# Moving eight conditioning columns from TensorE to VectorE, and three re-timings around them

## The chip, the cores and the metric

One core of a Trainium2 chip. The metric is device time of one launch in microseconds (us), median over runs. A chunk is 512 of the 2048 rows. TensorE is the matrix engine (PE in the profile, PEld its weight load), VectorE is DVE, ScalarE ACT, GpSimd POOL, SyncE SP.

## The reference, cut to what matters

```python
mod = (silu(c) @ w_mod)            # 6 vectors of 1024: sa, ca, ga, sb, cb, gb
h = layernorm(x) * (1 + ca) + sa
x = x + ga * attention(h)          # 32 query heads, 4 key/value heads, last 512 keys
h = layernorm(x) * (1 + cb) + sb
x = x + gb * swiglu(h)
```

`x` is 2048 x 1024 in bf16. Every one of the six vectors is eight columns of 128 in the layout on the chip. The change is about `ga`, the gate of the attention output, first used when the output projection of the first half ends, some 265 us into the run.

## The kernel before

Attention runs in 64 head steps for each half of the rows, numbered 0 to 63 and 64 to 127. A step `i` projects a query, computes the scores of step `i - 1`, and multiplies the probabilities of step `i - 2` with the values. Each step has one softmax reciprocal on VectorE (L824), which serves below as its time mark. In the steps up to 20 the projection is a plain product; later ones use a seven-product scheme whose sums load VectorE. Small work is hung on the steps:

```python
def mod_mm(w_ap, wbuf, k, cols):           # a column of mod: weights 128x128 times one column
    for n, (j, o) in enumerate(cols):
        mm(bank(XB, 1, 2 * o), w_ap[:, j * P:(j + 1) * P], sc_bf[:, k:k + 1], ...)

def load_mt(n):                            # a 128-column block of w_mod, turned by the DMA crossbar
    T.op(Q_mt[n % 2], lambda: SP.dma_start_transpose(mt[n % 2]..., w_mod[:, (NF + n) * P:(NF + n + 1) * P]), ...)

def mod_col(n):                            # the same column on VectorE: multiply by silu(c), sum
    T.op(DVE, lambda: V.scalar_tensor_tensor(mt[n % 2], mt[n % 2], 1.0, sc_row, ..., accum_out=mcol[:, n:n + 1]), ...)

def row_task(dst, dbuf, src, sbuf):        # 8 columns -> a row on all partitions, in three parts
    ...                                    # 4 ScalarE diagonals, then twice: 4 matmuls, a VectorE copy

# in pre0(i), the beginning of step i of the first half:
if i in (8, 9):
    load_wga(i - 8)                        # plain loads, 1 MB each, for the columns of ga
if i in (8, 9):
    for dt in range(4 * (i - 8), 4 * (i - 8) + 4):
        modulate(hT[1], B_hT[1], dt, 0, 0, B_mode, x1_tiles)
...
if i == 5:
    bgx.append(row_task(sc_row, B_scr, sc_bf[:, :], B_sc))
for k in {12: (0, 1, 2), 13: (3, 4, 5), 14: (6, 7)}.get(i, ()):
    mod_mm(wga[:, k, :], B_wga[k], k, GCOLS)
```

The output projection issues the big load of summed weights (`wo_sum`, 2 MB) after its first product, and lets background work, the normalization of the next rows, run between products:

```python
for ch in (2, 3):
    bg.append(ln_task(ch, 0, 0, B_mode))   # normalize a tile (L427), turn it by DMA; two tile buffers
o_phase(0, o_hook0)                        # o_hook0 runs one part of bg at a time

def hk(idx, j):                            # in o_phase
    if j == TPC - 1 and idx < 4:
        load(idx + 2)                      # idx 0: the first wo_sum load
```

The softmax here doesn't subtract the row's maximum and nothing guards it: scores larger than these inputs give would overflow.

## Time and profile before

| | before |
|---|---|
| median, range | 1160.27 us, 1159.91 to 1160.35 (3 runs) |
| TensorE busy | 1148.3 us, 99% of the span |
| VectorE busy | 817.4 us, 71% |
| weighted sums on VectorE (L603) | 24, 29.2 us |

The busy table tells who can set the time; the waits of TensorE, one by one, tell where anything is to be had besides its own work. Line numbers are those of each kernel: L805, L824, L827, L835, L956, L603 and L1122 before are L792, L811, L814, L822, L943, L590 and L1109 after.

### The profile page before, as it was taken

Reading aid. Unit: us, or ns where it says so; the run is one execution under the profiler, and the core shown is the slowest. Engines: PE = TensorE matmul, PEld = TensorE weight load, DVE = VectorE, ACT = ScalarE, POOL = GpSimd, SP = SyncE. Lnnn points to the kernel's source line nnn. Section 1 sums busy time; section 2 is a strip of 40 time slices with the busy share of each in tenths; the row PEclk is TensorE's granted clock in tenths of the full one; section 3 lists DMA queues with packets and bytes.
Section 4 is the critical chain, followed back from the end, with each engine's and each line's share of the span. In section 5 each row is a group of like instructions: output and inputs, shape, how many; then the busy total and the mean of one; then the engine's idle time right before and its main releaser. Section 6 shows DMA issues by size and latency. Waiting matters only on the chain.

```text
span 1158.3 us, 18250 instructions
## 1 busy us (share of the span) xinstructions
PE 1148.3 (99%) x7105; PEld 588.0 (51%) x7105; DVE 817.4 (71%) x1638; ACT 532.7 (46%) x745; POOL 68.4 (6%) x137
## 2 busy tenths in 40 slices
PE   8999999999999999999999999999999999999999
PEld 5565556654445666656444444444444444444444
DVE  4858897757567777686567898777558777776536
ACT  3867777731127777787110354454110444544110
POOL 1100221100000111111000010000000000000000
PEclk9999999999999999999999999999999999999999
DMA  9679999976807898844875332323774424234443
GB/s 330 145 181 207 225 217 211 236 182 194 242 3 183 197 194 204 203 94 119 191 198 165 87 95 73 108 75 100 209 201 143 121 73 109 73 98 131 130 160 109
DMA packets 289941, 179.98 MB, mean 155 GB/s; under 512 B 130496, under 2 KB 278080, under 8 KB 289856
## 3 DMA queue, kind: packets, MB, share of 16 engines
q1 hardware_dynamic: 226880, 92.31, 35.5%
q10 hardware_dynamic: 54336, 55.05, 15.0%
q0 software_dynamic: 8640, 31.46, 9.3%
q8 instruction: 56, 0.92, 0.3%
q14 instruction: 29, 0.24, 0.1%
HBM read 128.45 MB, written 19.92 MB: 128 GB/s over the span
## 4 chain that ended last, share of the span: by engine, by line
PE 96%; DVE 2%; ACT 1%; DMA 1%; issue 0%; SPq 0%; ACTq 0%; DVEq 0%
PE ps L272 96%; ACT arena L805 1%; DMA arena<-in_A_wq_dram 1%; DVE arena L835 1%; DVE arena L906 0%; DVE st L413 0%; SPq L341 0%; SPq L310 0%; PE ps L276 0%; ACT arena L618 0%; DVE arena L852 0%; ACT tmp L743 0%; DVE arena L1566 0%; ACT L1551 0%; DVE arena L827 0%
## 5 line engine op out<-in xcount | busy, mean ns | idle before, releaser
L272 PE MATMUL ps<-arena 128*128 128x512 f16 (+2 forms) x6800 | 1141.2, 330 | 7.0 <-POOL arena L406 2.2
L272 PEld LDWEIGHTS ps<-arena 128*128 128x128 bf16 (+1 forms) x6800 | 577.8, 98 | 563.0 <-DVE arena L835 6.2
L805 ACT ACTIVATE arena<-ps 128x1024 bf16<-128x1024 f32 x256 | 261.5, 1022 | 44.6 <-PE ps L272 32.8
L838 ACT ACTIVATE tmp<-ps 128x512 f32<-128x512 f32 x167 | 99.7, 597 | 295.9 <-PE ps L272 280.8
L906 DVE TENSOR_TENSOR arena<-arena 128x512 f16<-128x512 bf16 x328 | 133.3, 419 | 3.0
L835 DVE TENSOR_TENSOR arena<-ps,tmp 128x512 bf16<-128x512 f32 (+1 forms) x134 | 91.8, 685 | 49.3 <-PE ps L272 37.8
L838 ACT ACTIVATE nsc<-ps 128x512 f32<-128x512 f32 x84 | 50.1, 596 | 93.2 <-PE ps L272 90.9
L827 DVE TENSOR_TENSOR arena<-ps,rl 128x512 f16<-128x512 f32 x128 | 88.5, 691 | 4.9 <-DVE rl L824 0.5
L835 DVE TENSOR_TENSOR arena<-ps,nsc 128x512 f16<-128x512 f32 x84 | 57.3, 687 | 41.2 <-PE ps L272 30.0
L824 DVE RECIPROCAL rl<-ps 128x4 f32<-128x4 f32 x128 | 23.1, 180 | 87.1 <-PE ps L272 86.2
L1551 ACT ACTIVATE arena<-arena 128x512 f16<-128x512 f16 x84 | 49.9, 624 | 32.4 <-DVE arena L835 32.4
L1122 DVE TENSOR_TENSOR tmp<-ps,tmp 128x512 f32<-128x512 f32 x32 | 22.1, 690 | 58.5 <-ACT tmp L838 48.8
L1046 DVE TENSOR_TENSOR arena<-arena 128x2048 f16<-128x2048 f16 (+3 forms) x56 | 56.0, 1010 | 9.3 <-PE ps L272 8.8
L838 ACT ACTIVATE arena<-ps 128x512 f32<-128x512 f32 x16 | 9.6, 597 | 90.5 <-PE ps L272 90.5
L956 DVE TENSOR_TENSOR arena<-arena 128x512 f16<-128x512 bf16 x120 | 47.9, 419 | 2.0 <-DMA arena<-in_A_wo_dram 0.9
L413 DVE BATCH_NORM_STATS2 st<-x_res 128x6 f32<-128x512 bf16 x58 | 39.5, 682 | 3.7 <-DMA x_res<-in_A_x_dram 3.5
L1566 DVE TENSOR_TENSOR arena<-arena 128x512 f16<-128x512 f16 x84 | 35.0, 416 | 0.3
L1123 DVE TENSOR_TENSOR tmp<-tmp,rowb 128x512 f32<-128x512 f32 (+1 forms) x49 | 33.7, 687 | 1.7
L427 DVE TENSOR_SCALAR nsc<-x_res,mv,rstd 128x1024 f16<-128x1024 bf16 (+1 forms) x30 | 16.2, 539 | 23.3 <-DMA arena<-nsc 22.4
L603 DVE SCALAR_TENSOR_TENSOR arena<-arena 128x1024 bf16<-128x1024 bf16 x24 | 29.2, 1215 | 0.0
L1124 DVE TENSOR_TENSOR arena<-tmp,x_res 128x512 bf16<-128x512 f32 (+1 forms) x33 | 22.3, 676 | 1.1
L835 DVE TENSOR_TENSOR arena<-ps,rowb 128x512 f16<-128x512 f32 x28 | 19.3, 690 | 3.9 <-ACT rowb L838 3.4
(87 smaller groups left out, 333.4 us busy)
## 6 DMA issues: line engine op xcount, KB each, us to landing
arena<-in_A_wq_dram SPq DMA_DIRECT2D x28, 512.0 KB, 5.3
arena<-wo_sum ACTq DMA_DIRECT2D x7, 2048.0 KB, 8.6
arena<-in_B_w_gate_dram SPq DMA_DIRECT2D x28, 512.0 KB, 4.0
arena<-in_B_w_up_dram SPq DMA_DIRECT2D x28, 512.0 KB, 5.1
arena<-wd_sum ACTq DMA_DIRECT2D x8, 1792.0 KB, 7.8
arena<-in_B_w_down_dram ACTq DMA_DIRECT2D x6, 1792.0 KB, 7.1
arena<-in_A_wo_dram POOLq DMA_DIRECT2D x16, 512.0 KB, 4.8
wo_sum<-arena POOLq DMA_DIRECT2D x16, 512.0 KB, 4.6
```

The costliest lines, as they stand in the source:

```text
L272: T.op(PE, lambda: TE.matmul(out_ap, lhsT, rhs, start=start, stop=stop, skip_group_check=skip), reads=reads, writes=[bank_buf])
L413: T.op(DVE, lambda: V.bn_stats(st_[sl][:, hf * 6:hf * 6 + 6], x_res[:, t, hf * 512:hf * 512 + 512]), reads=[B_x[t]], writes=[B_st[sl]])
L805: T.op(ACT, lambda: A.activation(ex_s[es][:, 2 * kp:2 * kp + 2, :], banks2(SCB + 2 * kp), AF.Exp, scale=att_scale), writes=[PB[SCB + 2 * k ...
L827: T.op(DVE, lambda: V.tensor_tensor(o_s[os_].rearrange("p (a b) d -> p a b d", a=2), psap(PVB * 512, [[512, 2], [130, 2], [1, P]]), rlb, A ...
L835: T.op(DVE, lambda: V.tensor_tensor(out, bank(ba), other, ADD), reads=[ob2], writes=[PB[ba], ob])
L838: T.op(ACT, lambda: A.activation(dst, bank(bk), AF.Copy), writes=[PB[bk], db])
L906: T.op(st, lambda: eng.tensor_tensor(o, a, b, op), reads=rd, writes=[wr])
L956: T.op(DVE, lambda: V.tensor_tensor(o, a, b, SUB), reads=rd, writes=[wr])
L1046: T.op(DVE, lambda: V.tensor_tensor(o, a, b, SUB), reads=rd, writes=[sb])
L1123: T.op(DVE, lambda: V.tensor_tensor(tm, tm, rw, MULT), reads=[B_row[row]], writes=[tb])
L1551: T.op(ACT, lambda: A.activation(o, s_, AF.Silu), reads=[sb], writes=[ob])
L1566: T.op(DVE, lambda: V.tensor_tensor(gu[blk][:, p, :], o, s_, MULT), reads=[sb, ob], writes=[B_gu[blk][p]])
```

## The change

Its intent: TensorE sets the time, so the 64 one-column matmuls for `ga` go; `ga` is computed like the other late columns, from crossbar-turned weights and VectorE sums, placed in steps where VectorE has room. The row of silu(c) that these sums need is spread at step 8 instead of 5, chunk 1 is scaled six tiles then two, and the `ga` row is spread later.

```diff
-            NF = NE + DT
-            NL = NJ - NF
+            NL = NJ - NE
...
-            LOADT = {14 + 4 * n: n for n in range(NL)}
+            TAKES = [12, 17, 61] + [i for i in range(15, 2 * NI - 15) if i % 4 == 3 or (i > NI + 2 and i % 4 == 2 and i % 5 in (1, 4))]
+            TAKES = sorted(TAKES)[:NL]
+            TAKET = {i: n for n, i in enumerate(TAKES)}
+            LOADT = {max(i - 4, TAKES[max(n - 2, 0)] if n > 1 else 0): n for i, n in TAKET.items()}
...
-                        mod_take(g0, B_late[g0 + 1])
-                        if g0 == 1:
+                        mod_take(g0, B_late[g0])
+                        if g0 == 0:
+                            bgx.append(row_task(rowb[0], B_row[0], mod_bf[:, 2 * DT:3 * DT], B_late[0]))
+                        elif g0 == 2:
...
-                if i in (8, 9):
-                    load_wga(i - 8)
...
-                    for dt in range(4 * (i - 8), 4 * (i - 8) + 4):
+                    for dt in range(6 * (i - 8), 6 if i == 8 else DT):
...
-                if i == 5:
+                if i == 8:
                     bgx.append(row_task(sc_row, B_scr, sc_bf[:, :], B_sc))
-                for k in {12: (0, 1, 2), 13: (3, 4, 5), 14: (6, 7)}.get(i, ()):
-                    mod_mm(wga[:, k, :], B_wga[k], k, GCOLS)
```

More of the change, by code (lines that the diff above doesn't have):

```diff
@@ L188, in bass_adaLN_cond__sliding_block_cached__swiglu_ffn__prompt_kernel @@
     c6 = S_("c6", [P, DT], F32)
-    mcol = S_("mcol", [P, 3 * DT], F32)
+    mcol = S_("mcol", [P, 4 * DT], F32)
     gain = [S_("gain%d" % i, [P, DT], BF16) for i in range(2)]
@@ L572, in _ @@
             norm(2, 2, 2, 512, 512)
-            B_wga = [_Buf("wga%d" % k) for k in range(DT)]
-            wga = arena.at(OFF_OT[3], [DT, D], BF16, B_wga)
-            GCOLS = [(j, j) for j in range(DT)]
-            def load_wga(i):
-                T.op(dq("q_wga%d" % i), lambda: SP.dma_start(
-                    wga[:, i * HK:(i + 1) * HK, :],
-                    w_mod[i * HK * P:(i + 1) * HK * P, NE * P:NE * P + D].rearrange("(k p) n -> p k n", p=P)),
-                     writes=B_wga[i * HK:(i + 1) * HK])
-            NF = NE + DT
-            NL = NJ - NF
+            NL = NJ - NE
             B_mt = [_Buf("mt%d" % i) for i in range(2)]
@@ L598, in load_mt @@
                 T.op(Q_mt[n % 2], lambda: SP.dma_start_transpose(
-                    mt[n % 2].rearrange("p (a b) -> p a b", a=1), w_mod[:, (NF + n) * P:(NF + n + 1) * P]),
+                    mt[n % 2].rearrange("p (a b) -> p a b", a=1), w_mod[:, (NE + n) * P:(NE + n + 1) * P]),
                      writes=[B_mt[n % 2]])
@@ L607, in mod_take @@
             def mod_take(g0, cbuf):
-                T.op(DVE, lambda: V.tensor_copy(mod_bf[:, NF + g0 * DT:NF + (g0 + 1) * DT], mcol[:, g0 * DT:(g0 + 1) * DT]),
+                T.op(DVE, lambda: V.tensor_copy(mod_bf[:, NE + g0 * DT:NE + (g0 + 1) * DT], mcol[:, g0 * DT:(g0 + 1) * DT]),
                      reads=[B_mcol], writes=[cbuf])
@@ L1194, in _ @@
             LOADX = {14: 2, 20: 3}
-            LOADT = {14 + 4 * n: n for n in range(NL)}
+            TAKES = [12, 17, 61] + [i for i in range(15, 2 * NI - 15) if i % 4 == 3 or (i > NI + 2 and i % 4 == 2 and i % 5 in (1, 4))]
+            TAKES = sorted(TAKES)[:NL]
+            TAKET = {i: n for n, i in enumerate(TAKES)}
+            LOADT = {max(i - 4, TAKES[max(n - 2, 0)] if n > 1 else 0): n for i, n in TAKET.items()}
+            assert len(TAKES) == NL and len(LOADT) == NL and not {NI, NI + 1} & (set(TAKET) | set(LOADT))
             take_oT(0)
@@ L1220, in mods @@
             def mods(i):
-                if i - 5 in LOADT:
-                    n = LOADT[i - 5]
+                if i in TAKET:
+                    n = TAKET[i]
                     mod_col(n)
@@ L1225, in mods @@
                     if last == DT - 1:
-                        mod_take(g0, B_late[g0 + 1])
-                        if g0 == 1:
+                        mod_take(g0, B_late[g0])
+                        if g0 == 0:
+                            bgx.append(row_task(rowb[0], B_row[0], mod_bf[:, 2 * DT:3 * DT], B_late[0]))
+                        elif g0 == 2:
                             mod_gain(1, B_late[2], B_g[1])
-                        elif g0 == 2:
+                        elif g0 == 3:
                             bgx.append(row_task(rowb[1], B_row[1], mod_bf[:, 5 * DT:6 * DT], B_late[3]))
@@ L1271, in pre0 @@
                     next(x1_stats[1])
-                if i == 5:
+                if i == 8:
                     bgx.append(row_task(sc_row, B_scr, sc_bf[:, :], B_sc))
-                for k in {12: (0, 1, 2), 13: (3, 4, 5), 14: (6, 7)}.get(i, ()):
-                    mod_mm(wga[:, k, :], B_wga[k], k, GCOLS)
-                    if k == DT - 1:
-                        T.op(DVE, lambda: V.tensor_copy(mod_bf[:, NE:NF], psap(XB * 512, [[2, DT]])), writes=[PB[XB], B_late[0]])
-                        bgx.append(row_task(rowb[0], B_row[0], mod_bf[:, NE:NF], B_late[0]))
                 if i == ND + 2:
```

## The prediction

> **What bounds the kernel now.** I read three views, in this order: the page's busy table and chain that ended last (which engine sets the end), then TensorE's timeline of the first 125 us (where that engine is held up, and by whom), then the timeline of all engines from 45 to 80 us (what the others do there). The page first:
>
> ```profile
> span 1158.3 us, 18250 instructions
> ...
> PE 1148.3 (99%) x7105; PEld 588.0 (51%) x7105; DVE 817.4 (71%) x1638; ACT 532.7 (46%) x745; POOL 68.4 (6%) x137
> ...
> PE 96%; DVE 2%; ACT 1%; DMA 1%; issue 0%; SPq 0%; ACTq 0%; DVEq 0%
> ```
>
> TensorE is busy 99% of the span and carries 96% of the last chain. So a change can save only two things: work that TensorE itself does, and the few moments in which it stands. TensorE's timeline of the early attention steps shows both:
>
> ```profile
> 47.53 0.60 PE L272 MATMUL ps<-arena 128*128 128x512 bf16 x2 [0.24 <-ACT arena L805]
> 48.65 6.09 PE L272 MATMUL ps<-arena 128*128 128x512 bf16 x54 [0.51 <-ACT arena L805]
> 55.20 11.90 PE L272 MATMUL ps<-arena 128*128 128x512 f16 x88 [0.46 <-DVE arena L432]
> 66.94 0.74 PE L272 MATMUL ps<-sc_bf,arena 128*128 128x1 bf16 x24
> 67.55 3.66 PE L272 MATMUL ps<-arena 128*128 128x512 bf16 x28
> 71.04 0.74 PE L272 MATMUL ps<-sc_bf,arena 128*128 128x1 bf16 x24
> 71.64 3.66 PE L272 MATMUL ps<-arena 128*128 128x512 bf16 x28
> 75.14 0.54 PE L272 MATMUL ps<-sc_bf,arena 128*128 128x1 bf16 x16
> 75.54 23.79 PE L272 MATMUL ps<-arena 128*128 128x512 bf16 x198
> ```
>
> Columns: start, duration, instruction, count, and in brackets the idle time before it with what ended it. The reader is to see the 24+24+16 = 64 one-column matmuls (output 128x1), which are the gate columns and which the change deletes; two waits on ScalarE's exponential (L805) at 47.5 and 48.7; and one wait at 55.20 on the scaling of chunk 1 (L432, `modulate`). The all-engine timeline says what stands behind them:
>
> ```profile
> 45.29 1.28 ACT L618 ACTIVATE arena<-arena,c 128x128 bf16<-128x128 bf16 x4
> ...
> 46.48 2.12 ACT L805 ACTIVATE arena<-ps 128x1024 bf16<-128x1024 f32 x2
> ...
> 48.49 1.27 ACT L618 ACTIVATE arena<-arena,c 128x128 bf16<-128x128 bf16 x4
> ...
> 51.02 0.68 DVE L626 CAST arena<-ps 128x512 bf16<-128x512 f32 x1
> 51.62 1.37 DVE L432 TENSOR_SCALAR arena<-arena,gain,mod_bf 128x512 f16<-128x512 f16 x4
> ...
> 54.13 0.69 DVE L827 TENSOR_TENSOR arena<-ps,rl 128x512 f16<-128x512 f32 x1
> 54.74 1.42 DVE L432 TENSOR_SCALAR arena<-arena,gain,mod_bf 128x512 f16<-128x512 f16 x4
> ```
>
> The L618 rows are the diagonals of the conditioning row (`row_task`), the L626 row its copy: they sit in ScalarE's and VectorE's queues ahead of exponentials and scalings. VectorE does four scalings in step 8 and four in step 9, the latter only after its softmax division (L827); TensorE needs them at once.
>
> **What the Trainium skill says.** "TensorE: Matmul & The Clock Gate", section "Back-to-back issue gap", gives an issue floor of about 25 ns for matmuls of 1 to 64 columns. The trace agrees: 67.55 - 66.94 = 0.61 us for 24, 25.4 ns each. The 163 ns that a row shows as the mean of one is latency, not cost. "VectorE: DVE Perf Modes", section "The perf-mode tier table", lists 2x for tensor_tensor on bf16 in SBUF but has no row for scalar_tensor_tensor with an accumulated sum; here one over 1024 elements takes 1215 ns (L603, 24 of them, 29.2 us), plus 82 ns to read the sum. "Advanced Engine Details and Errata", section "X-Bar Transpose (TRN2)", says transposing DMAs are as fast as plain ones; here a crossbar load of one 256 KB weight column block lands 4.4 us (median, 3.1 to 10.8) after issue, a plain 256 KB load of the same weights 6.5, so nothing contradicts it.
>
> **The change, part by part.**
>
> 1. Gate columns off TensorE. 64 matmuls go. The pitch of an attention step, read from one softmax reciprocal to the next in the timeline, is 3.50 us without columns (58.42, 61.92, 65.42) and 4.09, 4.10 and 3.90 us with them (69.51, 73.61, 77.51). 0.59 + 0.60 + 0.40 = **1.59 us**, 24.8 ns each, all on the path.
>
> 2. The same columns on VectorE: 8 more weighted sums of 1.215 + 0.08 us = 10.4 us, and one 0.17 us copy in place of the one removed. By the diff's formula the 32 sums fall in steps 12, 15, 17, then 19, 23, 27 and so on; against before the new places are 12, 15, 17, 61, 74, 86, 94, 106. I compared each with VectorE's busy time in that step: steps 12 to 18 hold 1.6 to 3.1 us of 3.5, and step 17 loses the old row copy as well; step 61 has 1.6 of 2.6; steps 74, 86, 94, 106 have about 2.1 of 3.5, so 3.4 after. The steps where VectorE is truly full (23 to 42; five small TensorE waits on L835 lie there) keep exactly the sums they had. Hence about **0**, and I allow 0.1 us. The change deletes 2 MB of plain loads at steps 8 and 9 and adds eight 256 KB crossbar loads, the same bytes spread out. Every sum comes at least four steps (11.6 us or more, by the reciprocals of steps 59 and 63) after its load was placed, against a slowest landing of 10.8: hidden, but not by much in the steps with short pitch.
>
> 3. First conditioning row (`sc_row`) from steps 5 to 7 to steps 8 to 10. Its 8 small matmuls cost the same 0.44 us anywhere (a step with four of them is 3.72 instead of 3.50). What changes is ScalarE. TensorE's start-to-start pitch at the two waits exceeds the normal 0.21 us by 0.41 and 0.68, 1.09 us together. Without the diagonals the two exponentials (2.13 us) still limit the short step 7: replaying the queue, the exponential at 46.48 begins at about 45.75 and the second half of the next scores at 47.9 instead of 48.65, of which 0.22 is moved row work. Gain **0.54 us**, not 1.09. At steps 8 to 10 ScalarE has 1.36 us free per 3.5 us step against diagonals of 1.28 to 1.48: no new wait.
>
> 4. Six scalings in step 8, two in step 9. At 55.20 and the next three matmul groups starts slip by 0.63 + 0.11 + 0.11 + 0.16 = 1.01 us, because four scalings at 0.34 us each run after the division. With six done earlier (2.06 us, and the copies at 47.93 and 51.02 gone from VectorE's queue) only two run late; I replay them ending 0.24 us after TensorE would want the last. Gain **0.78 us**. The crossbar transposes that feed the scalings land by 48.2, before they would start at about 50.1.
>
> 5. Gate row (`rowb[0]`) from steps 14 to 16 to steps 40, 44, 48. Same matmuls. ScalarE has 10.6 us of work per 13.1 us group there, so 1.48 us fits, but tightly within one step. The copy of eight columns (0.17 us) at step 39 lands where VectorE is full: cost **0.2**, with 0.1 more for ScalarE.
>
> Sum: 1.59 + 0.54 + 0.78 - 0.1 - 0.3 = 2.5 us. I take 2.4: 1160.27 - 2.4 = **1157.9 us**, 0.2%.
>
> **Rivals.**
> *VectorE becomes the wait.* 10.4 us more work on an engine that TensorE does wait for. For it: step 111, where a sum, its copy and statistics meet, is followed by a 0.44 us wait on L835. Against: the new places have room on paper. If each of the five second-half and late places cost such a wait, 2.2 us go back: about 1160.
> *Only the matmuls count.* If ScalarE's two exponentials hold the early short steps anyway and the scalings stay late behind something I missed, such as the transposes, parts 3 and 4 give nothing: 1160.27 - 1.6 + 0.4 = 1159.1.
> *Crossbar loads crowd the DMA queues.* DMA is 95 to 100% busy between 78 and 245 us. A late load stalls VectorE's in-order queue and then TensorE: 1 to 3 us, so up to 1161. Against: only 2 of the extra loads fall after 210 us in chunk 0, and no TensorE wait there names a DMA.
> *More than predicted.* If all waits of parts 3 and 4 vanish: 1.59 + 1.09 + 1.01 = 3.7, about 1156.6. Against: the two exponentials of 2.13 us do not fit the short step.
>
> **Range and chances.** Ends of the range: nearly everything of parts 3 and 4 gained and nothing lost (1156.8), and only the matmuls with small VectorE losses (1159.2). Runs of before spread over 0.44 us, so the machine adds little. 2% would be 23 us; the whole stretch that changes holds no such sum. Same: 0.99.
>
> **What would show it.** In the profile after: no one-column matmuls between 66 and 76 us and reciprocals 3.50 us apart there (part 1); 32 rows of L603's kind (39 us) with no new wait on L835 near steps 61, 74, 86, 94, 106 (part 2); one wait of about 0.4 to 0.6 us on the exponential near 48 us, not two (part 3); the wait on the scaling at about 0.25 us (part 4); the wait on L835 near step 40 grown by about 0.2 us (part 5). A wait of VectorE on the crossbar loads, or several waits on L835 in the second chunk, would make it wrong.

## The result, and the profile after

The changed kernel takes 1158.79 us (median of 6, 1157.90 to 1159.89) against 1160.31 us before in the same rounds (1159.84 to 1160.84). The ratio is 0.9988, 95% interval 0.9975 to 1.0000. Ratios here are the mean time of one kernel's fast runs over that of the other's of the same rounds, so not quite the ratio of the medians. That is 1.5 us where 2.4 was predicted, inside the range.

The page of the changed kernel, its busy line and one of its groups:

```profile
PE 1147.0 (99%) x7041; PEld 586.2 (51%) x7041; DVE 826.1 (71%) x1654; ACT 532.7 (46%) x745; POOL 69.1 (6%) x137
...
L590 DVE SCALAR_TENSOR_TENSOR arena<-arena 128x1024 bf16<-128x1024 bf16 x32 | 38.9, 1215 | 0.0
```

64 matmuls are gone (7105 to 7041) and eight sums came (24 to 32). TensorE's timeline from 40 to 125 us, then the lines of its continuation from 125 to 172 us (start, duration, what, count, idle time before and what ended it):

```profile
...
42.27 5.44 PE L272 MATMUL ps<-arena 128*128 128x512 bf16 x48 [0.16 <-ACT arena L792]
48.17 48.15 PE L272 MATMUL ps<-arena 128*128 128x512 bf16 x392 [0.46 <-ACT arena L792]
96.79 11.14 PE L272 MATMUL ps<-arena 128*128 128x512 bf16 x98 [0.46 <-ACT arena L792]
...
```

```profile
...
149.01 17.02 PE L272 MATMUL ps<-arena 128*128 128x512 f16 x140 [0.66 <-DVE arena L822]
166.23 5.96 PE L272 MATMUL ps<-arena 128*128 128x512 f16 x46 [0.20 <-DVE arena L822]
```

Before, TensorE's timeline from 125 to 175 us is one row:

```profile
124.83 50.53 PE L272 MATMUL ps<-arena 128*128 128x512 f16 x407
```

The reader is to see that the stretch which held two waits, the scaling wait and the columns is now one unbroken row of 48 us with one wait ahead of it, and that new or larger waits stand at 149 and 166 us. To see what each is worth, I lined up the softmax reciprocals of equal steps in the two traces:

| stretch (reciprocals of steps) | before, us | after, us | difference |
|---|---|---|---|
| start to 4 | 41.24 | 41.52 | +0.28 |
| 4 to 20 | 57.69 | 54.41 | -3.28 |
| 20 to 34 | 45.33 | 45.36 | +0.03 |
| 34 to 46 | 39.89 | 41.13 | +1.24 |
| 46 to 65 | 60.88 | 60.87 | -0.01 |
| 65 to 66 (holds the output projection) | 102.89 | 103.40 | +0.51 |
| 66 to 129 | 206.28 | 206.18 | -0.10 |
| 129 to the end | 604.09 | 604.08 | -0.01 |

So the change gains 3.28 us by step 20 and gives 1.75 us back at two places far from it (0.44 of it are the gate row's own matmuls, which moved from steps 14 to 16 to steps 40 and 44). The start is not the change's: both kernels are the same there, and it lay between -0.4 and +1.8 us of before in later traces (TensorE's first matmuls wait for a load, and its first half-size ones sometimes run at 213 ns instead of 109). I therefore compare traces from the reciprocal of step 4 to the end of the span: 1117.05 us before, 1115.43 after.

The timeline of VectorE around the first place given back, changed kernel, 141 to 151 us:

```profile
143.58 0.88 DVE L943 TENSOR_TENSOR arena<-arena 128x512 f16<-128x512 bf16 x2 [0.34 <-DMA arena<-in_A_wo_dram]
...
144.99 1.21 DVE L590 SCALAR_TENSOR_TENSOR arena<-arena 128x1024 bf16<-128x1024 bf16 x1
146.12 0.08 DVE L590 DVE_READ_ACCUMULATOR arena<-arena 128x1 f32 x1
146.24 0.17 DVE L595 CAST mod_bf<-mcol 128x8 bf16<-128x8 f32 x1
```

The copy of the eight finished columns (L595) sits in a step in which VectorE has no room, and here the weight sums (L943) also came late, as a weight load held VectorE for 0.34 us.

The second place, in the output projection. All-engine timelines, before (252 to 270 us) and after (250 to 268 us):

```profile
251.73 18.51 PE L272 MATMUL ps<-arena 128*128 128x512 bf16 x85
...
252.84 0.54 DVE L427 TENSOR_SCALAR nsc<-x_res,mv,rstd 128x1024 f16<-128x1024 bf16 x1
...
259.36 0.55 DVE L427 TENSOR_SCALAR nsc<-x_res,mv,rstd 128x1024 f16<-128x1024 bf16 x1 [0.74 <-DMA arena<-nsc]
...
264.00 0.55 DVE L427 TENSOR_SCALAR nsc<-x_res,mv,rstd 128x1024 f16<-128x1024 bf16 x1 [1.70 <-DMA arena<-nsc]
264.46 0.68 DVE L1122 TENSOR_TENSOR tmp<-ps,tmp 128x512 f32<-128x512 f32 x1
...
```

```profile
254.06 0.54 DVE L427 TENSOR_SCALAR nsc<-x_res,mv,rstd 128x1024 f16<-128x1024 bf16 x1
...
262.62 0.55 DVE L427 TENSOR_SCALAR nsc<-x_res,mv,rstd 128x1024 f16<-128x1024 bf16 x1 [2.78 <-DMA arena<-nsc]
...
265.93 0.68 DVE L1109 TENSOR_TENSOR tmp<-ps,tmp 128x512 f32<-128x512 f32 x1
...
266.67 1.69 PE L272 MATMUL ps<-arena 128*128 128x512 f16 x7 [0.32 <-DVE tmp L1109]
```

The third normalization (L427) needs the tile buffer of the first, which its transpose still reads. In the changed kernel that transpose landed later, VectorE stood 2.78 us there, and its sum L1109 released TensorE's bank (the buffer that its next product goes to) late. The kernel before also waits on such transposes, 0.74 and then 1.70 us, without cost to TensorE. Against step 65, its first normalization (L427) starts at 7.8 us and its sum L1122 at 19.4; in the changed kernel these are 10.8 and 22.6. So VectorE's later start, after the last attention transposes, makes most of the difference between these two traces; whether it is needed for the wait is tested below. The question for the experiments: which part of the change does this, and is it chance?

### The profile page after: what moved, and what is told of

Its sections match the earlier page's. It is cut to its first block, busy times and chain, and to the rows that moved or that the text cites. A ratio compares the mean times of both kernels' runs of the same rounds, so it can differ in the third digit from the quotient of the medians.

```text
span 1156.9 us, 18141 instructions
## 1 busy us (share of the span) xinstructions
PE 1147.0 (99%) x7041; PEld 586.2 (51%) x7041; DVE 826.1 (71%) x1654; ACT 532.7 (46%) x745; POOL 69.1 (6%) x137
## 4 chain that ended last, share of the span: by engine, by line
PE 95%; DVE 2%; DMA 1%; ACT 1%; issue 1%; SPq 0%; DVEq 0%; ACTq 0%
PE ps L272 95%; DMA arena<-nsc 1%; DVE arena L822 1%; DMA arena<-in_A_wq_dram 1%; ACT arena L792 0%; DVE arena L893 0%; DVE st L413 0%; SPq L341 0%; SPq L310 0%; PE ps L276 0%; DVE arena L1049 0%; DVE arena L839 0%; DVE nsc L427 0%; DVE arena L1552 0%; DVE arena L943 0%
## 5 line engine op out<-in xcount | busy, mean ns | idle before, releaser
L1109 DVE TENSOR_TENSOR tmp<-ps,tmp 128x512 f32<-128x512 f32 x32 | 22.1, 689 | 62.1 <-ACT tmp L825 52.4
L943 DVE TENSOR_TENSOR arena<-arena 128x512 f16<-128x512 bf16 x120 | 47.8, 419 | 1.4 <-DMA arena<-in_A_wo_dram 0.3
L590 DVE SCALAR_TENSOR_TENSOR arena<-arena 128x1024 bf16<-128x1024 bf16 x32 | 38.9, 1215 | 0.0
L427 DVE TENSOR_SCALAR nsc<-x_res,mv,rstd 128x1024 f16<-128x1024 bf16 (+1 forms) x30 | 16.1, 538 | 19.5 <-DMA arena<-nsc 18.7
L1111 DVE TENSOR_TENSOR arena<-tmp,x_res 128x512 bf16<-128x512 f32 (+1 forms) x33 | 22.3, 675 | 1.1
```

Of the source, the lines that this page charges most:

```text
L943: T.op(DVE, lambda: V.tensor_tensor(o, a, b, SUB), reads=rd, writes=[wr])
```

## The experiments

Up to four kernels on one chip. All results were correct; `free_cols` uses the wrong columns on purpose and passed the comparison all the same. The column "from step 4" is the measure named above; "wait" is by how much TensorE's start-to-start pitch at L1109 (L1122) exceeds the normal 0.21 us; "fetch" is when the instruction fetch nearest to the output projection started and "wo_sum" when that load landed, both in us after the reciprocal of step 65, from the trace's DMA records (for the fetch, the 16 KB ones alone).

| kernel | median (runs) | ratio, 95% | from step 4 | wait | fetch | wo_sum |
|---|---|---|---|---|---|---|
| before | 1160.31 (6) | | 1117.05 | none | 1.6 | 18.3 |
| before_again | 1160.37 (5) | 1.0001, 0.9989 to 1.0014 | 1117.35 | none | 1.9 | 18.2 |
| sched_only | 1159.07 (5) | 0.9986, 0.9973 to 0.9999 | 1115.85 | none | 1.7 | 17.8 |
| after | 1158.79 (6) | 0.9988, 0.9975 to 1.0000 | 1115.43 | 0.49 | 9.7 | 18.7 |
| again | 1158.19 (5) | 0.9983, 0.9970 to 0.9995 | 1115.76 | 1.20 | 9.8 | 19.4 |
| cols_only | 1159.99 (5) | 0.9993, 0.9980 to 1.0007 | 1116.11 | 0.40 | 9.7 | 18.9 |
| free_cols | 1158.68 (5) | 0.9982, 0.9970 to 0.9995 | 1115.45 | 0.93 | 10.0 | 19.7 |
| load66 | 1158.21 (5) | 0.9985, 0.9972 to 0.9999 | 1115.50 | 0.91 | 10.3 | 19.7 |
| late_row | 1157.66 (5) | 0.9978, 0.9965 to 0.9991 | 1115.08 | 0.89 | 10.2 | 19.0 |
| scale44 | 1160.17 (1) | | 1116.78 | 0.51 | 9.6 | 19.0 |
| norm_early | 1158.08 (5) | 0.9980, 0.9968 to 0.9993 | 1114.59 | none | 9.5 | 18.3 |
| pad32 | 1159.84 (5) | 0.9981, 0.9967 to 0.9995 | 1115.41 | none | 4.7 | 18.4 |
| pad64 | 1159.11 (1) | | 1115.39 | none | 2.8 | 17.5 |
| best_ne | 1157.62 (5) | 0.9967, 0.9954 to 0.9979 | 1114.01 | none | 12.0 | 18.6 |

**before_again**: the kernel before, as if it were a change.

> The kernel before, submitted as if it were a change: ratio 1.000; its distance from 1 is the noise of such a comparison. Its second trace shows whether the first output projection, free of a wait in the first trace of before, is so in every execution (theory A: the wait on L1122 comes from the change alone), or waits there at times too (theory B: the place is a race of transfers in either kernel, decided by a microsecond).

The ratio is 1.0001 and known to about 0.13%, 1.5 us. There is no wait at L1122 in its trace either. Most differences between variants are smaller than that, so times alone do not order them; their traces do, step by step, as the stretches outside a named place repeat within some hundredths of a us, save single slips of 0.4 to 1.0 us at step 24 or steps 51 to 57 in four of the traces, `before_again` among them, whose cause I did not follow.

**again**: the changed kernel, once more, on another chip.

> The changed kernel once more. If the two VectorE waits that gave time back (0.8 us on L822 near step 35, 0.5 us on L1109 in the first output projection) belong to the change, they are in this trace too, and the time is 1.2 to 1.9 us under before. If they were chance of one execution's transfers, they are gone or elsewhere.

Both waits are there: 0.51 us of excess at step 36 (0.82 in the first trace) and 1.20 at L1109. They belong to the change; their sizes vary. From step 4 the trace is 1.28 us under before; the ratio says 2.0 us, just past the 1.2 to 1.9 expected, with 1.5 us of noise.

**sched_only**: the kernel before with the two re-timings alone.

```diff
-                    for dt in range(4 * (i - 8), 4 * (i - 8) + 4):
+                    for dt in range(6 * (i - 8), 6 if i == 8 else DT):
-                if i == 5:
+                if i == 8:
```

> Only the conditioning row at step 8 and the scalings 6+2; the columns stay on TensorE. Predicted 0.54 + 0.78 = 1.3 us under before; by the first trace 1.2. Rival (the waits only move): 0.

From step 4 it takes 1.20 us less than before (1.50 less than `before_again`), all of it by step 12, and nothing comes back. Predicted 1.3: it holds.

**cols_only**: the changed kernel with those two lines as before.

> The columns on VectorE and the late gate row, but the conditioning row at step 5 and the scalings 4+4, as before. If the steps add up as predicted: 64 matmuls less (1.59 us) minus what is given back later (1.3 us by the first trace): 0.2 to 0.5 us under before. Rival (the columns alone carry the gain): 1.4 us under before.

By the traces 0.94 us under before, which is neither the 0.2 to 0.5 expected nor the rival's 1.4: 1.6 gained at steps 12 to 14, 0.37 lost around steps 36 and 41, 0.40 lost at L1109, and 0.1 gained at step 111. Outside the output projection the prediction's parts are separate and add: without the waits at L1109, 1.34 us here and 1.20 in `sched_only` stand against 2.48 in `again`. The time (ratio 0.9993) can't tell 0.5 from 1.4.

**free_cols**: `sched_only` without any computation of the gate columns.

```diff
-                if i in (8, 9):
-                    load_wga(i - 8)
-                for k in {12: (0, 1, 2), 13: (3, 4, 5), 14: (6, 7)}.get(i, ()):
-                    mod_mm(wga[:, k, :], B_wga[k], k, GCOLS)
-                    ...
+                if i == 14:
+                    bgx.append(row_task(rowb[0], B_row[0], mod_bf[:, 0:DT], B_mode))
```

> As sched_only, and the gate columns are simply not computed (the gate row is spread from other columns, so the result is wrong on purpose): no matmuls, no sums, no loads for them. The most that the change could give: 1.59 us under sched_only, 2.8 us under before. The distance from here to the changed kernel is what the new place of the columns costs; the first trace says 1.3 us, my prediction said 0.4.

A miss that taught most. Up to step 16 it gains the 1.60 us over `sched_only`, as expected. But it too loses 0.93 us in the output projection (there the sum is L1122), though it has no additional crossbar load and no additional sum (its timeline, 250 to 268 us):

```profile
265.88 0.68 DVE L1122 TENSOR_TENSOR tmp<-ps,tmp 128x512 f32<-128x512 f32 x1
...
266.62 1.68 PE L272 MATMUL ps<-arena 128*128 128x512 f16 x7 [0.76 <-DVE tmp L1122]
```

So neither of these is needed for the wait. What it shares with the changed kernel is that TensorE has 64 matmuls less and that the two 1 MB loads of steps 8 and 9 are gone.

**load66**: the changed kernel, one crossbar load later.

```diff
+            del LOADT[63]
+            LOADT[66] = 16
```

> The changed kernel with the one crossbar load of step 63 moved to step 66, out of the way of the last transposes of attention outputs. Theory A (that load delays them by 2 to 3 us and VectorE with them): the last transpose lands 5 to 6 us after the last attention step instead of 8, the wait on L1109 is gone, 0.4 to 1.2 us faster than the changed kernel. Theory B (the landing of the big wo_sum load decides): the transposes are early but the wait on L1109 stays in some executions, as in free_cols, which lacked this load and waited 0.9 us.

The last transposes of attention outputs land 6.4 us after step 65 instead of 8.1, and the wait is still 0.91 us. Theory A fails: the crowding that I had named as a rival is real in most traces (the last of those transposes lands at 5.6 to 9.0 us where the load of step 63 is there, at 5.2 to 6.4 where it isn't) but the wait does not need it.

**late_row**: the changed kernel with the copy and the row of `ga` put off from step 35 to 45.

```diff
-                        mod_take(g0, B_late[g0])
-                        if g0 == 0:
-                            bgx.append(row_task(rowb[0], B_row[0], mod_bf[:, 2 * DT:3 * DT], B_late[0]))
-                        elif g0 == 2:
+                        if g0:
+                            mod_take(g0, B_late[g0])
+                        if g0 == 2:
...
+                if i == 45:
+                    mod_take(0, B_late[0])
+                    bgx.append(row_task(rowb[0], B_row[0], mod_bf[:, 2 * DT:3 * DT], B_late[0]))
```

> The changed kernel with the copy of the gate columns and the spreading of the gate row put off from step 35 to step 45, past the steps in which VectorE is full. The wait at step 36 goes back to the 0.31 us of before and the one near step 41 (0.37) is gone or as before (0.19): 0.3 to 0.4 us faster than the changed kernel up to the end of the first attention half. If the row's ScalarE work is what costs, a new wait shows at steps 48 to 53 instead.

TensorE's timeline from 125 to 220 us, where the changed kernel had 0.66 and 0.20:

```profile
...
148.20 72.00 PE L272 MATMUL ps<-arena 128*128 128x512 f16 x590 [0.15 <-DVE arena L822]
```

Steps 34 to 46 take 39.90 us, as before the change, and no new wait shows later; 0.45 us between steps 50 and 60 is its 8 row matmuls, moved there. `again` took 40.71 us for steps 34 to 46; less 0.44 for its row matmuls, `late_row` gains 0.37 us.

**norm_early**: the changed kernel, first two normalizations ahead of the output projection's sums.

```diff
                 bg.append(ln_task(ch, 0, 0, B_mode))
+            run_bg(2)
             o_phase(0, o_hook0)
```

> The changed kernel with the first two normalizations of the next chunk (L427) issued before the sums of the output projection, so that their transposes are ahead of the wo_sum load in the queue. If the chain is wo_sum load, then transpose of the first normalized tile, then VectorE's third normalization, then L1109, the wait is gone with the crossbar load still in place: the third normalization starts well before 19.4 us after the last attention step, 0.5 to 1.2 us faster than the changed kernel. If only late attention-output transposes matter, the wait stays.

The crossbar load and the late attention transposes (8.0 us) are still there, and the wait is gone: 102.90 us from step 65 to 66, as before, and from step 4 it takes 0.84 us less than `after` and 1.17 less than `again`, in the range expected. The timeline of `norm_early` from 241 to 270 us has the normalizations at

```profile
243.36 0.99 DVE L427 TENSOR_SCALAR nsc<-x_res,mv,rstd 128x1024 f16<-128x1024 bf16 x2
...
253.18 0.54 DVE L427 TENSOR_SCALAR nsc<-x_res,mv,rstd 128x1024 f16<-128x1024 bf16 x1
```

with no wait on a transpose. The two transposes, issued ahead of the load, land at 8.9 and 9.6 us after step 65 instead of 19.2 and 20.0. The chain is shown: wo_sum load and the transposes beside it, VectorE's third normalization, L1109, TensorE. Over the traces without this edit, the third transpose is issued 19.8 to 20.6 us after step 65 in the seven that wait, and 14.9 to 18.8 in the five that don't. The sum at L1109 (L1122 or L1111 in other kernels) tells how near they are: in the seven its start, 22.5 to 23.4 us after step 65, is always the wait plus 22.15 us. In the five it starts with 0.6 (`pad64`), 0.7 (`sched_only`), 1.6 and 2.7 (both traces of before) and 2.6 us (`pad32`) to spare.

**pad32 and pad64**: what do 64 missing matmuls do 170 us later? The DMA view of the wo_sum load, from issue to landing, before (253.87 to 263.33 us), after (252.14 to 261.95 us) and `pad32` (254.13 to 263.67 us), lists its queues; the third is a fetch of instructions:

```profile
q10 hardware_dynamic: 2064, 2.10, 68.6%
q1 hardware_dynamic: 2319, 0.58, 33.7%
```

```profile
q10 hardware_dynamic: 2064, 2.10, 67.7%
q1 hardware_dynamic: 1299, 0.32, 32.0%
q8 instruction: 1, 0.02, 0.9%
```

```profile
q10 hardware_dynamic: 2064, 2.10, 66.9%
q1 hardware_dynamic: 2260, 0.56, 31.1%
```

The columns are packets, MB and share of 16 engines. One 16 KB fetch falls into the load only after the change. The Trainium skill, "Advanced Engine Details and Errata", section "ISA Cache", gives instruction cache lines of 16 KB, 256 instructions; the trace agrees on the size (q8 on the page before: 56 packets, 0.92 MB). The hypothesis is that a stream that is shorter ahead of a point takes its next line at another time. To test it, matmuls without effect go back where TensorE waits for its first weights anyway:

```diff
+            for _ in range(32):          # 64 in pad64
+                mm(bank(WB, 1), zwarm[:, 0:P], zwarm[:, 0:1], True, True, [B_zw], PB[WB])
             for kc in range(HK):
                 for h in range(3):
                     q_first(h, kc, 0, 2 * P)
```

> The changed kernel with 32 one-column matmuls added where TensorE waits for its first weights at 11 us, nothing else. Theory C: deleting 64 matmuls shortened TensorE's instruction stream, so that one fetch of 16 KB of instructions moved from 1.6 to 9.7-10.3 us after the last attention step, into the wo_sum load, whose landing slips by about 1 us, and with it the transposes and L1109. Then half as many matmuls put back move the fetch to about 5 to 6 us, the wo_sum load lands by 18.5, and the wait on L1109 (0.4 to 1.2 us) is gone: 0.4 to 1.2 us faster than the changed kernel, although TensorE has more to do. Theory A or chance: the fetch does not move or the wait stays, and the time is that of the changed kernel.

> As pad32, with 64 one-column matmuls, as many as the change deleted. Theory C (the place of the instruction fetch follows the number of TensorE's instructions): the fetch of 9.7 us, which 32 moved to 4.7, goes to about 0 to 2 us after the last attention step, where before has it (1.6 to 1.9), the next one comes after 20 us, and TensorE has no wait on L1109, as in both traces of before. If pad32 was chance, the fetch is elsewhere or the wait is back.

The fetch moved from 9.7 to 4.7 and to 2.8 us (I had said 0 to 2 for the last), and the next one came at 24.4 in `pad64`. The load landed at 18.4 and 17.5 us, and TensorE has no wait on L1109 in either. So the number of TensorE's instructions places the fetch, and with the fetch ahead of the load the wait is gone, in one trace each; the two 1 MB loads stayed deleted.

The two traces are not equal evidence. In `pad32` the first normalized tile's transpose was issued 0.1 us before the load, as in the first trace of before, and landed at 14.4 us; that order alone could have cured the wait. In `pad64` it was issued 1.8 us behind the load, and the wait was missed by 0.6 us. The cleanest pair is `sched_only` and `free_cols`: first transposes issued at 9.2 us, loads at 8.85, and the load landed at 17.8 us with the fetch at 1.7, at 19.7 with the fetch inside it.

What isn't shown is whether the fetch itself holds the load up, and how one packet of 16 KB could delay 2 MB: in the DMA views of `load66` and `free_cols` the rate dips to 94 and 21 GB/s for a slice or more, some 4 us after the fetch began; in that of `after` there is no such dip within the load. Nor is the fetch alone enough: in `norm_early` it starts at 9.5 us and the load, with fewer transposes beside it, lands at 18.3.

The times of the padded kernels gain nothing, against 0.4 to 1.2 us expected of `pad32`: `pad32` began 1.8 us later and slipped by 0.63 us at step 51, `pad64` lost 1.04 us at step 35 (0.20 of it is the change's own), where a late weight load held VectorE for 0.76 us.

**scale44**: the changed kernel with the scalings 4+4, one look.

> The changed kernel with the scalings 4+4 and the conditioning row at step 8. If the 6+2 split is what removed the waits at step 9, about 0.7 us comes back there as waits on L432; if it was the conditioning row's copies leaving VectorE's queue, nearly nothing comes back.

TensorE's timeline from 46 to 58 us:

```profile
...
48.26 5.87 PE L272 MATMUL ps<-arena 128*128 128x512 bf16 x50 [0.46 <-ACT arena L792]
54.60 3.62 PE L272 MATMUL ps<-arena 128*128 128x512 f16 x29 [0.46 <-DVE arena L432]
```

The wait on the scaling is back in full: 0.63 + 0.11 + 0.11 + 0.16 = 1.01 us of slips, as before the change, against 0.29 with 6+2. The split does it, and the row's copies leaving VectorE's queue alone do nothing.

**best_ne**: `late_row` and `norm_early` together.

> late_row and norm_early together: the gate row at step 45 and the first two normalizations ahead. The two gains lie in different stretches and should add: 0.37 us before the output projection and 0.4 to 1.2 us in it; 1157.2 to 1157.6, the fastest of all so far.

1157.62 us (1157.08 to 1157.88), at the edge of the 1157.2 to 1157.6 expected, level with `late_row` (1157.66) and 3.4 us under before in its rounds; from step 4 it takes 1.42 us less than `after` and 1.75 less than `again`. It beats the kernel before beyond noise. Against the changed kernel the traces say so; the two ratios come from different chips and their intervals meet (0.9954 to 0.9979, 0.9975 to 1.0000).

## Why the prediction was right or wrong

The mechanism and the range held; the sum was 0.9 us too hopeful against the medians. The time alone could not have told: its interval covers gains from 0 to 2.9 us, and the noise of a comparison is 1.5 us, not the 0.44 us of spread that the prediction goes by. What follows rests on the traces.

1. Columns off TensorE: 1.59 predicted. Reciprocals of steps 11 to 14 are now 3.50 us apart (64.46, 67.96, 71.46, 74.95): 10.49 us instead of 12.09, 1.60. Right.
2. Eight more sums: about 0 predicted. The stretch from step 66 to 110 repeats within 0.01 us (144.36 us in both traces), with VectorE at 3.4 of 3.5 us in the new places. Right.
3. Conditioning row at step 8: 0.54 predicted, two waits to become one. One is left, of 0.63 us excess where 1.09 was: 0.46. Right.
4. Scalings 6+2: 0.78 predicted, 0.24 of wait to remain. 0.29 remains, 0.21 of it on the projection's copy (L643) that now stands behind six scalings: 0.72 gained. Right, and `scale44` shows the cause.
5. Gate row: I misread the list of steps by one. The eighth column is summed at step 35, not 39, and the row is spread at 36, 40 and 44. The cost predicted was 0.2 + 0.1. In `again`, `cols_only`, `load66` and `norm_early` it is 0.19 at step 36 and 0.18 beyond the row's own matmuls at step 41, 0.37 in all: nearly right. In the first trace it is 0.8, as a weight load for the sums came 0.34 us late in the same step.
6. The step that failed is the sum's silent last term: that nothing happens in the output projection. I had read that no TensorE wait there names a DMA, and concluded that transfers there are free. TensorE indeed never waits for a DMA there; VectorE does, at one place for 2.78 us, and TensorE for VectorE, 0.40 to 1.20 us in the seven traces that lack the 64 matmuls and have the normalizations in their old place. My rival "crossbar loads crowd the DMA queues" had the right path (a late transfer, then VectorE, then TensorE) and the wrong cause.

With 3.28 by step 20 less the gate row's 0.44 of matmuls, which come back later, 2.84 stands against my 2.91; less 0.37 to 0.8 and 0.4 to 1.2, that makes 0.8 to 2.1 us, and 1.5 was measured.

## What to carry to other kernels

Work that left the bounding engine paid its full issue time here (1.60 us for 64 matmuls), and could be counted from the pitch of the steps; what came back came at places with a thin margin, far away. So look in the profile for engines that wait just short of holding the bounding one: a chain of VectorE behind a transfer, with 0.6 to 2.7 us to spare, was turned into a TensorE wait by a shift that no dependency explains. When two transfers share the queues and only one has a deadline, issue that one first: two normalizations moved ahead of a 2 MB load cured it in both traces that have the edit, with the fetch still inside the load.

## What the Trainium skill lacked or had wrong

- "Advanced Engine Details and Errata", section "ISA Cache": the 16 KB lines agree with the fetches seen (56 packets, 0.92 MB). It lacks what a fetch goes along with where it falls into a transfer: with the fetch at 9.6 to 10.3 us, inside a 2 MB load, the load landed at 18.7 to 19.7 us; with it at 1.6 to 4.7 us, at 17.5 to 18.4. With fewer transposes beside the load the difference was small (fetch at 9.5 and 12.0 us, landing at 18.3 and 18.6).
- "VectorE: DVE Perf Modes", section "The perf-mode tier table": no row for scalar_tensor_tensor with an accumulated sum. Here 1215 ns for 1024 bf16 elements in SBUF, and 82 ns for reading the sum.
- "Advanced Engine Details and Errata", section "X-Bar Transpose (TRN2)": it calls transposing DMAs as fast as regular ones and gives a bandwidth. It lacks landing times in company: the 256 KB transpose of a normalized tile landed 3.1 us after issue alone and 4.8 to 10.5 us after it when issued while the wo_sum load ran.
